# First phase of a fused adaLN transformer block: two row tiles normalized on GpSimd, ScalarE's sum ahead of a copy, first query weights in two transfers

## The chip, the cores and the metric

The kernel runs on one core of a Trainium2 chip. The metric is the device time of one execution in microseconds (us). An execution varies from run to run (six runs of the kernel before: 1272.22 to 1273.15 us), so small differences below are means over runs of the same job (the same chip, the same minutes), with two standard errors behind "±". TensorE is called PE, VectorE DVE, ScalarE ACT and GpSimd POOL, as in the profile.

## The reference, cut to what matters

```python
mod = silu(c) @ w_mod                      # sa, ca, ga, sb, cb, gb: six vectors of 1024
h = layernorm(x) * (1 + ca) + sa           # x: 2048 x 1024
x = x + ga * attention(h, k_cache, v_cache, wq, wo)    # 32 query heads, 4 kv heads, last 512 keys
h = layernorm(x) * (1 + cb) + sb
x = x + gb * swiglu(h, w_gate, w_up, w_down)
```

Only the start matters here: before the first query matmul, PE needs x normalized and transposed for the first 512 rows (four row tiles of 128), the vector ca, and query weights. The shift sa is folded in later as a bias.

## The kernel before: the parts concerned

All transfers are issued in this order on one queue (tile `wm` holds columns of w_mod, `wq8`, which the profile prints as `wq`, the query weights of the first eight heads):

```python
for tt in range(QT): load_x(tt)            # 4 x 256 KB
for half in range(DH):
    load_wm(1, half)                       # scale ca: 1 MB
    load_wq8(2 * half)                     # 512 KB
    load_wq8(2 * half + 1)                 # 512 KB
load_wm(0, 0); ...; load_wm(0, 1)          # shift sa: 2 x 1 MB
```

The first phase, with cuts marked:

```python
nc.tensor.transpose(sil_ps, sil_r, ident[0:DT, 0:DT])
nc.scalar.copy(out=siluc, in_=sil_ps)      # silu(c) as a column, for the w_mod matmuls
warm(4)                                    # filler matmuls
...
stats_0(0)                # DVE: mean and variance of row tile 0
act_sum(1)                # ACT: sum of row tile 1
rstd_0(0)                 # ACT
stats_0(2)                # DVE
act_squares(1)            # ACT
warm(3)
xpose_0(0, ln_norm(0))    # DVE normalizes, PE transposes (8 matmuls)
rstd_0(1, 1.0 / D); rstd_0(2)
warm(5)
stats_0(3)
xpose_0(1, ln_norm(1)); xpose_0(2, ln_norm(2))
rstd_0(3)
n3 = ln_norm(3)
mod_cols(1, 0, ca1, True, (0,))            # first columns of ca: 8 matmuls of one column
xpose_0(3, n3)
...                                        # DVE scales h; then query matmuls, first half
mod_cols(1, 1, ca1, True)                  # second half of ca, after 20 query matmuls
...
q0(1, (6, 7)); sa_mm(0, (0, 1)); q0(2, (6, 7)); sa_mm(0, (2, 3)); sa_out(0)
q0(3, (6, 7)); sh_mm(0, range(5)); q0(4, (6, 7)); sh_mm(0, (5, 6))
sa_mm(1, (0,)); q0(5, (6, 7)); sa_mm(1, (1, 2, 3)); sa_out(1)   # shift sa
```

The order of every engine's instructions in this phase is pinned.

Of the kernel before, what the change touches and what calls it, by code (L numbers as in the profile page):

```python
# [9 lines left out]
ALU = mybir.AluOpType  # L10
AX = mybir.AxisListType
BF16 = mybir.dt.bfloat16
# [576 lines left out]
def fast_path(ctx, tc, flag, A_x, A_k_cache, A_v_cache, A_wq, A_wo, B_x, B_w_gate, B_w_up,  # L589
# [3 lines left out]
    nc = tc.nc  # L593
    P = 128
    _, S, D = A_x.shape
# [23 lines left out]
    wq_v = A_wq.rearrange("(dt p) n -> p dt n", p=P)  # L619
# [15 lines left out]
    wk = ctx.enter_context(tc.tile_pool(name="work", bufs=2))  # L635
# [7 lines left out]
    def blkB(name, shape, dt=BF16):  # L643
        return pb_.tile(shape, dt, name=name, tag="B")
# [4 lines left out]
    def mm(name, shape=(P, 512), dt=FP32):  # L649
        return psp.tile(list(shape), dt, name=name, tag="mm", bufs=4)  # L650

    def big(name, shape=(P, 2, 512), dt=FP32):
        return psp.tile(list(shape), dt, name=name, tag="s", bufs=2)
# [6 lines left out]
    def pin(ins, what="steps"):  # L660
        return tc.keep_in_program_order(ins) if stage[what] else ins

    def fetch(out, in_):
        pin(nc.sync.dma_start(out=out, in_=in_), "dma")

    def load(out, in_):
        with nc.allow_non_contiguous_dma(reason="weight slice"):
            fetch(out=out, in_=in_)
# [18 lines left out]
    xt = [xpool.tile([P, D], BF16, name=f"x{tt}", tag=f"x{tt}") for tt in range(S // P)]  # L687
# [21 lines left out]

    def load_wq8(i):  # L710
        t = blkB("wq8", [P, 2, 8 * P])
        load(t, wq_v[:, 2 * i:2 * i + 2, 0:8 * P])
        wq8.append(t)

    for tt in range(QT):
# [1 line left out]
    for half in range(DH):  # L717
        load_wm(1, half)
        load_wq8(2 * half)
        load_wq8(2 * half + 1)  # L720
# [35 lines left out]
    def warm(n):  # L756
        for _ in range(n):
            nc.tensor.matmul(warm_ps, lhsT=ones_bf, rhs=warm_w, start=True, stop=True)
# [15 lines left out]
    siluc = const.tile([P, DT], BF16, name="siluc")  # L774
    sil_ps = mm("sil_ps", (P, DT), BF16)
    nc.tensor.transpose(sil_ps, sil_r, ident[0:DT, 0:DT])
    nc.scalar.copy(out=siluc, in_=sil_ps)
    warm(4)

    def mod_cols(vec, half, dst, add_one, tiles=(0, 1, 2, 3)):  # L780
# [59 lines left out]
    ln = {}  # L840

    def ln_stats(tt, late=None):
        st = sm.tile([P, DH, nc.vector.BN_STATS_DIM], FP32, name="st", tag="st")
        for i in range(DH):
            pin(nc.vector.bn_stats(out=st[:, i, :], in_=xt[tt][:, i * 512:(i + 1) * 512]))  # L845
        if late is not None:
            nc.vector.bn_aggr(out=late[:, 0:2], in_=st)
            return
        mv = sm.tile([P, 4], FP32, name="mv", tag="mv", bufs=4)
        nc.vector.bn_aggr(out=mv[:, 0:2], in_=st)  # L850
        nc.scalar.activation(out=mv[:, 2:3], in_=mv[:, 1:2], func=ACT.Ln, bias=eps_t)
        nc.scalar.activation(out=mv[:, 2:3], in_=mv[:, 2:3], func=ACT.Exp, scale=-0.5)
        ln[tt] = mv

    def ln_norm(tt, on_act=False, n=None):
        mv = ln.pop(tt)
        n = wk.tile([P, D], BF16, name="xn", tag="xn", bufs=3) if n is None else n
        if on_act:
            nc.vector.scalar_tensor_tensor(out=mv[:, 3:4], in0=mv[:, 0:1], scalar=-1.0,
                                           in1=mv[:, 2:3], op0=ALU.mult, op1=ALU.mult)  # L860
            nc.scalar.activation(out=n, in_=xt[tt], func=ACT.Identity, bias=mv[:, 3:4],
                                 scale=mv[:, 2:3])
        else:
            pin(nc.vector.tensor_scalar(out=n, in0=xt[tt], scalar1=mv[:, 0:1],
                                        scalar2=mv[:, 2:3], op0=ALU.subtract, op1=ALU.mult))
        return n

    xn = {}
# [89 lines left out]
    def xpose_0(t, n):  # L958
        for dt in range(DT):
            nc.tensor.transpose(h0_ps[dt // 4][:, dt % 4, t * P:(t + 1) * P],  # L960
                                n[:, dt * P:(dt + 1) * P], ident)

    def rstd_0(t, sums=1.0):
        mv = ln[t]
        nc.scalar.activation(out=mv[:, 2:3], in_=mv[:, 1:2], func=ACT.Ln, bias=eps_t, scale=sums)
        nc.scalar.activation(out=mv[:, 2:3], in_=mv[:, 2:3], func=ACT.Exp, scale=-0.5)

    def stats_0(t):
        mv = ln[t] = sm.tile([P, 4], FP32, name="mv", tag="mv", bufs=4)
        ln_stats(t, mv)  # L970

    def act_sum(t):
        mv = ln[t] = sm.tile([P, 4], FP32, name="mv", tag="mv", bufs=4)
        junk = wk.tile([P, D], BF16, name="junk", tag="junk", bufs=1)
        nc.scalar.activation(out=junk, in_=xt[t], func=ACT.Identity, accum_out=mv[:, 3:4])

    def act_squares(t):
# [3 lines left out]
        nc.scalar.activation(out=junk, in_=xt[t], func=ACT.Square, bias=mv[:, 0:1], scale=-1.0,  # L981
                             accum_out=mv[:, 1:2])

    stats_0(0)
    act_sum(1)
    rstd_0(0)
    stats_0(2)
    act_squares(1)
    warm(3)
    xpose_0(0, ln_norm(0))  # L990
    rstd_0(1, 1.0 / D)
    rstd_0(2)
    warm(5)
    stats_0(3)
    xpose_0(1, ln_norm(1))
    xpose_0(2, ln_norm(2))
    rstd_0(3)
    n3 = ln_norm(3)
# [63 lines left out]
    for i in range(2):  # L1062
        t = big("q_ps")
# [228 lines left out]
    for tt in range(QT, S // P):  # L1292
        cc, t = divmod(tt, QT)
# [98 lines left out]
    for cc in range(NTC):  # L1392
# [3 lines left out]
        for fg in range(NFG):  # L1396
            n = cc * NFG + fg + 1
# [32 lines left out]
def kernel(tc, *args):  # L1430
    nc = tc.nc
    with tc.tile_pool(name="guard", bufs=1) as gp:
        flag = gp.tile([1, 1], I32, name="flag")
        over = fast_path(tc, flag, *args)
        with tc.If(over > 0):
            general_path(tc, *args)
# [30 lines left out]
```

## Time and profile before

| | before |
|---|---|
| median of 3 runs | 1272.88 us |
| span of the profiled run | 1271.2 us |
| PE busy | 1263.8 us |
| tile 2 of x lands; first half of the ca columns lands | 6.07; 9.77 us |
| first query matmul | 12.12 us |
| first score matmul (phase over, PE packed from here) | 30.61 us |

A landing is the last of the sixteen completion records of a transfer in the trace. The timeline's columns are start, duration, engine, line, operation, tiles and shapes, count and, in brackets, the idle time in front and what ended it. The places where PE first meets a large transfer look like this:

```profile
10.81 0.30 PEld L785 LDWEIGHTS <-wm 128*128 128x128 bf16 x8
12.12 4.60 PE L1032 MATMUL q_ps<-hs,wq 128*128 128x512 bf16 x20
16.34 1.06 PEld L785 LDWEIGHTS <-wm 128*128 128x128 bf16 x32
22.75 0.67 PEld L1050 LDWEIGHTS <-wm 128*128 128x128 bf16 x16
30.61 0.59 PE L1197 MATMUL s_ps<-qT,kT 128*128 128x512 bf16 x2
```

No bracket says "<-DMA". PE meets each of these tiles after it has landed.

### The profile page before, as it was taken

How to read it: one execution, taken by the hardware profiler on the slowest of the kernel's cores; microseconds unless marked ns; L12 is line 12 of the kernel's file. 1: busy time of each engine (PE TensorE's matmuls, PEld its weight loads, DVE VectorE, ACT ScalarE, POOL GpSimd, SP SyncE). 2: the span in 40 equal slices, each digit the busy share in tenths (PEclk: the TensorE clock that was granted, in tenths of full speed). 3: DMA queues.
4: the chain of work that ended last, by engine and by line, in shares of the span. 5: the costliest groups of instructions: out<-in, count | busy, mean ns of one | idle time of the engine just before them, and what ended most of it. 6: DMA issues, size and time to landing. Idle time of an engine off the chain costs nothing.

```text
span 1271.2 us, 18164 instructions
## 1 busy us (share of the span) xinstructions
PE 1263.8 (99%) x7589; PEld 641.3 (50%) x7589; DVE 609.8 (48%) x1334; ACT 335.6 (26%) x440; POOL 1.4 (0%) x11
## 2 busy tenths in 40 slices
PE   9999999999999999999999999999999999999998
PEld 4555555555555555555554444444444444444444
DVE  5666658885678665567564631321122112221122
ACT  3643334343333433334341111011100111011100
POOL 0000000000000000000000000000000000000000
PEclk9999999999999999999999999999999999999999
DMA  9897656779557655455575478336633565425702
GB/s 291 205 250 176 173 141 155 185 159 217 127 137 173 152 137 154 113 154 108 125 202 147 133 227 250 95 94 209 213 116 105 168 210 185 158 91 168 246 19 67
DMA packets 306844, 204.46 MB, mean 161 GB/s; under 512 B 145601, under 2 KB 303297, under 8 KB 306754
## 3 DMA queue, kind: packets, MB, share of 16 engines
q1 hardware_dynamic: 301842, 199.03, 58.0%
q10 hardware_dynamic: 4912, 4.20, 1.0%
q8 instruction: 61, 1.00, 0.3%
q14 instruction: 29, 0.24, 0.1%
HBM read 165.94 MB, written 4.21 MB: 134 GB/s over the span
## 4 chain that ended last, share of the span: by engine, by line
PE 97%; DVE 2%; DMA 0%; SPq 0%; issue 0%
PE gu_ps L1343 30%; PE a_ps L1261 17%; PE q_ps L1186 16%; PE d_ps L1363 15%; PE o_ps L1229 9%; PE s_ps L1197 8%; PE q_ps L1032 1%; DVE st L845 0%; DMA x<-in_A_x_dram 0%; DVE junk L1120 0%; DVE junk L816 0%; DVE oq L1216 0%; DVE qT L946 0%; DVE f L1274 0%; DVE f L1273 0%; DVE x L1276 0%
## 5 line engine op out<-in xcount | busy, mean ns | idle before, releaser
L1199 ACT ACTIVATE pT<-s_ps 128x1024 bf16<-128x1024 f32 x256 | 249.2, 1020 | 345.0 <-PE s_ps L1197 344.9
L1261 PE MATMUL a_ps<-wo,oT 128*128 128x512 bf16 x1024 | 241.9, 379 | 0.0
L1186 PE MATMUL q_ps<-hT,wq 128*128 128x512 bf16 x960 | 227.1, 379 | 0.0
L1349 DVE TENSOR_TENSOR guT<-gu_ps,sg 128x512 bf16<-128x512 f32 x112 | 77.5, 692 | 287.5 <-ACT sg L1348 287.5
L1343 PE MATMUL gu_ps<-hT,wg 128*128 128x512 bf16 x896 | 211.7, 379 | 0.0
L1348 ACT ACTIVATE sg<-gu_ps 128x512 bf16<-128x512 f32 x112 | 66.9, 597 | 488.6 <-PE gu_ps L1343 480.1
L1363 PE MATMUL d_ps<-wd,guT 128*128 128x512 bf16 (+2 forms) x952 | 194.2, 366 | 0.0
L1343 PE MATMUL gu_ps<-hT,wu 128*128 128x512 bf16 x672 | 163.3, 379 | 0.0
L1261 PEld LDWEIGHTS <-oT 128*128 128x128 bf16 x1024 | 100.2, 98 | 120.6
L946 DVE CAST qT<-q_ps 128x512 bf16<-128x512 f32 x121 | 83.6, 691 | 151.7 <-PE q_ps L1186 151.4
L1186 PEld LDWEIGHTS <-wq 128*128 128x128 bf16 x960 | 93.9, 98 | 113.0
L1363 PEld LDWEIGHTS <-guT 128*128 128x128 bf16 x952 | 90.9, 98 | 103.0
L1229 PEld LDWEIGHTS <-pT 128*128 128x128 bf16 x2048 | 126.6, 98 | 30.5 <-issue 0.4
L1343 PEld LDWEIGHTS <-wg 128*128 128x128 bf16 x896 | 87.6, 98 | 105.5
L1229 PE MATMUL o_ps<-v_sb,pT 128*128 128x130 bf16 x2048 | 137.0, 220 | 0.1
L1197 PE MATMUL s_ps<-qT,kT 128*128 128x512 bf16 x512 | 131.6, 379 | 0.0
L1343 PEld LDWEIGHTS <-wu 128*128 128x128 bf16 x672 | 65.8, 98 | 79.3
L1216 DVE TENSOR_TENSOR oq<-o_ps,rl 128x256 bf16<-128x256 f32 (+2 forms) x256 | 100.5, 420 | 3.9
L1367 DVE TENSOR_TENSOR f<-d_ps,gb_bc 128x512 f32<-128x512 f32 (+2 forms) x34 | 22.5, 660 | 140.1 <-PE d_ps L1363 140.1
L1197 PEld LDWEIGHTS <-kT 128*128 128x128 bf16 x512 | 44.9, 98 | 31.2 <-issue 0.5
L1269 DVE TENSOR_TENSOR acc<-a_ps,acc 128x512 f32<-128x512 f32 x64 | 44.0, 688 | 32.6 <-PE a_ps L1261 32.6
L1343 PE MATMUL gu_ps<-hT,v_sb 128*128 128x512 bf16 x224 | 57.5, 379 | 0.0
(99 smaller groups left out, 426.4 us busy)
## 6 DMA issues: line engine op xcount, KB each, us to landing
wq<-in_A_wq_dram SPq DMA_DIRECT2D x64, 512.0 KB
wo<-in_A_wo_dram SPq DMA_DIRECT2D x64, 512.0 KB
wg<-in_B_w_gate_dram SPq DMA_DIRECT2D x56, 512.0 KB
wd<-in_B_w_down_dram SPq DMA_DIRECT2D x56, 512.0 KB
wu<-in_B_w_up_dram SPq DMA_DIRECT2D x42, 512.0 KB
v_sb<-in_B_w_up_dram SPq DMA_DIRECT2D x14, 512.0 KB
x<-in_A_x_dram SPq DMA_DIRECT2D x16, 256.0 KB
wm<-in_w_mod_dram SPq DMA_DIRECT2D x4, 1024.0 KB
```

Source lines behind the costliest of these rows:

```text
L946: nc.vector.tensor_copy(out=t, in_=q_ps)
L1186: nc.tensor.matmul(q_ps, lhsT=w, rhs=hT[("h1", cc)][:, dt, :], start=(dt == 0), stop=(dt == DT - 1))
L1197: nc.tensor.matmul(s_ps[:, i, :], lhsT=kT[:, kv, j * P:(j + 1) * P], rhs=qT[g], start=True, stop=True)
L1199: nc.scalar.activation(out=p[:, 2 * jj:2 * jj + 2, :], in_=s_ps, func=ACT.Exp, scale=scale)
L1216: nc.vector.tensor_tensor(out=dst, in0=ps[:, s0:s0 + cnt, 0:Dh], in1=sc, op=ALU.mult)
L1229: nc.tensor.matmul(o_slot["ps"][:, s_, :], lhsT=pT[g][:, j, t * P:(t + 1) * P], rhs=v_sb[:, kv, j, 0:VN], start=(j == 0), stop=(j == WT - 1))
L1261: nc.tensor.matmul(a_ps, lhsT=oT[(cc, 2 * q + i)][:, hh % 4, t * P:(t + 1) * P], rhs=wo_tiles[(cc, q, dh, i)][:, hh % 4, :], start=(hh == ...
L1269: nc.vector.tensor_tensor(out=acc[(cc, t)][:, dsl], in0=a_ps, in1=acc[(cc, t)][:, dsl], op=ALU.add)
L1343: nc.tensor.matmul(ps[:, n, :], lhsT=gu_w[(cc, fg, nm, dt // 4)][:, dt % 4, fi * P:(fi + 1) * P], rhs=hT[("h2", cc)][:, dt, :], start=(dt ...
L1348: nc.scalar.activation(out=g, in_=ps[:, 0, :], func=ACT.Silu)
L1349: nc.vector.tensor_tensor(out=guT[(cc, fg)][:, fi, :], in0=ps[:, 1, :], in1=g, op=ALU.mult)
L1363: nc.tensor.matmul(d_ps, lhsT=guT[(cc, f // 4)][:, f % 4, t * P:(t + 1) * P], rhs=wd_tiles[(cc, dh, f // 4)][:, f % 4, c0:c0 + w], start=( ...
```

## The change

DVE works through statistics and normalizations of four row tiles while POOL is idle. The change gives two of the normalizations to POOL, lets ACT start its sum before it waits for PE's silu(c), and cuts the first 512 KB of query weights in two so that PE can start on the first half.

```diff
     def load_wq8(i):
         t = blkB("wq8", [P, 2, 8 * P])
-        load(t, wq_v[:, 2 * i:2 * i + 2, 0:8 * P])
+        for j in range(2 * i, 2 * i + 2) if i == 0 else ():
+            load(t[:, j % 2, :], wq_v[:, j, 0:8 * P])
+        if i > 0:
+            load(t, wq_v[:, 2 * i:2 * i + 2, 0:8 * P])
 ...
-    nc.scalar.copy(out=siluc, in_=sil_ps)
     warm(4)
 ...
+    def norm_0(t):
+        mv = ln[t]
+        n = wk.tile([P, D], BF16, name="xn", tag="xn", bufs=3)
+        nc.gpsimd.tensor_scalar(out=mv[:, 3:4], in0=mv[:, 0:1], scalar1=-1.0, scalar2=1.0,
+                                op0=ALU.mult, op1=ALU.mult)
+        nc.gpsimd.tensor_scalar(out=n, in0=xt[t], scalar1=mv[:, 3:4], scalar2=mv[:, 2:3],
+                                op0=ALU.add, op1=ALU.mult)
+        return n
 ...
     act_sum(1)
+    nc.scalar.copy(out=siluc, in_=sil_ps)
 ...
-    xpose_0(0, ln_norm(0))
+    xpose_0(0, norm_0(0))
 ...
-    xpose_0(1, ln_norm(1))
+    xpose_0(1, norm_0(1))
```

## The prediction

> **What bounds the kernel now.** I read the page first, then the list of waits, then the timeline of the first 32 us, because the diff touches nothing after that. The page says that TensorE (PE) is busy almost everywhere, and the chain of work that ended last is almost all PE:
>
> ```profile
> PE 1263.8 (99%) x7589; PEld 641.3 (50%) x7589; DVE 609.8 (48%) x1334; ACT 335.6 (26%) x440; POOL 1.4 (0%) x11
> ...
> PE 97%; DVE 2%; DMA 0%; SPq 0%; issue 0%
> ```
>
> So 1271.2 - 1263.8 = 7.4 us of the span is all that PE does not fill. The 2% of DVE in the chain is not slack to be had everywhere: it lies at the start and at the very end. A change in the first phase can win only what makes the first query matmul (q_ps on tile hs) start sooner, and what PE then keeps. The chain in order of time shows the start:
>
> ```profile
> 1.67 4.40 DMA x<-in_A_x_dram
> 6.07 0.02 issue
> 6.09 1.30 DVE st L845 x2
> 7.39 0.02 issue
> 7.41 0.21 DVE mv L847
> 7.62 0.41 DVE xn L864
> 8.03 1.21 DVE st L845 x2
> 9.24 0.02 issue
> 9.26 0.04 DVE mv L847
> 9.30 0.09 issue
> 9.39 0.52 DVE xn L864
> 9.91 0.05 issue
> 9.95 1.08 PE h_ps L960 x16
> 11.03 0.18 PE mod_ps L785 x8
> 11.21 0.47 PE h_ps L960 x8
> 11.68 0.58 PE mod_ps L785 x24
> 12.26 4.46 PE q_ps L1032 x20
> ```
>
> The reader is to see that, from the landing of tile 2 of x at 6.07 to the transposes at 9.95, VectorE (DVE) does statistics and normalizations one after the other; only then does PE run as a chain. The first 4.6 us of it are the wait for x, which no part of the change touches. The timeline shows what DVE does there, columns start, duration, engine, line, operation:
>
> ```profile
> 7.54 0.49 DVE L864 TENSOR_SCALAR xn<-x,mv 128x1024 bf16<-128x1024 bf16 x1
> 7.95 1.28 DVE L845 BATCH_NORM_STATS2 st<-x 128x6 f32<-128x512 bf16 x2
> 9.26 0.21 DVE L847 BATCH_NORM_AGGREGATE mv<-st 128x2 f32<-128x12 f32 x1
> 9.39 1.42 DVE L864 TENSOR_SCALAR xn<-x,mv 128x1024 bf16<-128x1024 bf16 x3
> ```
>
> Row tile 0 is normalized ahead of tile 3's statistics, and tile 1 ahead of tiles 2 and 3. GpSimd (POOL) is idle all that time.
>
> The other side is DMA: in the windows from 4.4 to 23 us its share is 1.00 or more, at 349 to 373 GB/s. The completion records of the trace, last of sixteen per transfer, give the landings: x tile 1 at 3.94, tile 2 at 6.07, tile 3 at 6.73, scale columns wm (first half) at 9.77, first query weights at 11.28, second 12.69, second half of wm 15.66, the shift's two wm tiles 22.03 and 25.14. PE first uses these at 10.81, 12.10, about 13.5 (after six matmuls), 16.34, 22.75 and 25.91. **Each transfer that PE meets has only about 0.7 us in hand.**
>
> **What the Trainium skill says.** "GPSIMD Engine Reference", section 3.1, puts elementwise work with at most two operations and one input at 1.03 cycles an element at 1.2 GHz, a good unrolled loop at 1.8, two inputs at 2.6. For 1024 elements that is an estimate of 0.88, 1.54 or 2.2 us, plus dispatch. The trace before has no comparable instruction; POOL's 8x128 product took 0.42 us. "SBUF — State Buffer", section "Who interferes with whom", says that a DVE tensor_scalar in a two-port mode and a GpSimd instruction exclude each other, while DVE work with one SBUF input outside those modes does not contend. The normalizations (1024 elements in about 0.5 us, so over one element a cycle) are in such a mode by that page; the statistics (512 in 0.68 us) show one element or less. No overlap exists in the trace before. "TensorE: Matmul & The Clock Gate", Part 1, says that PE starts at half clock for a run-variable few microseconds: the trace agrees, the filler matmuls start 0.45 us apart until about 7.2 us and 0.22 to 0.25 after.
>
> **The change part by part.**
>
> *ScalarE order.* The sum of tile 1 (1.06 us) starts at 4.53 now, because ahead of it the copy of silu(c), 0.17 us, waited 1.29 us for PE. Tile 1 is there at 3.94, so the sum can start at about 3.96. The copy then follows, so rstd of tile 0 is ready 0.57 - 0.17 = 0.4 us sooner: 5.7 instead of 6.10. The squares and rstd of tile 1 move as well: ready at about 7.65 instead of 8.03. siluc itself comes at 5.2, long before its first reader at 10.8.
>
> *Rows 0 and 1 on GpSimd.* Adds two tiny negations (estimate 0.2 us each; the first one hides behind ScalarE's rstd) and two passes over 128x1024. I take 1.1 us each, the port-bound figure above plus about 0.2 of dispatch. Row 0: 5.8 to 6.9. Row 1 waits for its rstd at 7.65: 7.7 to 8.8. PE's filler (seven matmuls at half clock) ends at 7.44, so transposes of row 0 start at 7.45 instead of 8.09; five fillers (1.1 us) then run to 9.0, and row 1's transposes follow at once instead of at 9.95. By then neither is on the path.
>
> *DVE.* Loses two passes. Statistics of tile 3 start at 7.54 right behind tile 2's (now 7.95): 0.41 us. They and their aggregate end so that row 2 starts at 8.98 instead of 9.85 (the second of the three in the 9.39 group): 0.41 + 0.46 = 0.87 us sooner. Row 3 needs rstd of tile 3: the aggregate's start moves from 9.26 to 8.85, ScalarE's two steps from 9.50 to about 9.1, ready 9.63; row 3 is done at 10.18 instead of 10.81.
>
> *PE behind it.* Row 2's transposes 9.55 to 10.0; the first eight scale-column matmuls follow (wm landed 9.77, so just in time); row 3's transposes start at about 10.23 instead of 11.07. Gain here 0.84 us, and the scale of hs follows in the same spacing: first query matmul at about 11.28 instead of 12.12.
>
> *Weights in two pieces.* The first 256 KB hold all that the first three matmuls read. An x tile of that size took about 0.65 us, so it lands at 10.4 to 10.6 and the second at 11.28, as before. Without the split the 512 KB land at 11.28, which is just when hs is ready: the split is worth 0 to 0.1 us. It adds one issue on SP, off the path because the DMA queue is backed up.
>
> *What PE keeps.* With everything 0.84 us earlier, PE asks for the second half of wm at 15.50, which lands at 15.66 plus a few hundredths: kept gain 16.34 - 15.71 = 0.63. For the shift tiles: 22.75 - 22.08 = 0.67, 25.91 - 25.19 = 0.72, so these no longer cost more. The later kT lands at about 27.5 against a first use at 30.4. Sum: **-0.63 us**, rounded to -0.6, and PE stays the bound for the other 1240 us, where loads are issued by the release of buffers and move along with PE. 1272.88 - 0.6 = 1272.3 us.
>
> **Rivals.**
>
> 1. *GpSimd is slower than I take.* At 1.54 us plus dispatch, row 1 ends at about 9.4; row 2 on DVE would be blocked by the shared port from 8.98 to 9.4, row 3 ends near 10.5, the gain at the first query matmul is 0.5 us. At 2.2 us plus dispatch, row 0 ends at 8.1 and row 1 at 10.5, rows 2 and 3 are pushed to about 11.5, and the kernel loses some 0.4 us: 1273.3. For it: the 0.42 us for 128 elements is slow. Against: that one has two inputs, and the loop runs over one input with two operations.
> 2. *The gain is hidden by DMA.* The landings set a floor: if they come 0.3 us later in the run (the last of sixteen is over 1 us behind the first in each transfer, and a lagging DMA engine need not be the same), the kept gain falls to 0.3 us; if earlier, up to 0.84 us. That makes 1272.0 to 1272.6.
> 3. *The clock gate moves.* Fewer or shifted idle gaps of PE (0.65 us before the first transposes now) cannot cost much, but if full clock came 1 us later, the transposes would wait for fillers and the gain would be gone: about 1272.9.
>
> **Range and chances.** 60% for the 1.1 us pass (1271.9 to 1272.5), 25% for the middle case (1272.3 to 1272.7), 15% for the slow one (1273 to 1273.6). The three runs before spread over 0.63 us, which adds 0.3 either way. Predicted 1272.3, range 1271.7 to 1273.2. Two per cent are 25 us, over three times all of PE's idle time, so "faster" needs what does not exist, and a loss of 25 us would need waits far beyond this phase: 0.003 and 0.007.
>
> **What would show it right or wrong.** Right: POOL has two TENSOR_SCALAR passes of about 1.1 us before 9 us; ScalarE's sum starts near 4.0; statistics of tile 3 near 7.5; first q_ps matmul at 11.2 to 11.5; and PE waits a tenth or two for DMA ahead of the second-half mod_ps matmuls near 15.6, which it does not do now. Wrong: POOL passes of 2 us or more with DVE's row 2 late behind them (rival 1); a first q_ps matmul early but the score matmuls no earlier than 30.6 - 0.3 (rival 2); filler matmuls 0.45 us apart beyond 8 us (rival 3). The step I trust least is the GpSimd duration, next the DMA landings. It would be wrong as a whole if x landed differently in the changed kernel, since all of the chain hangs on tile 2 of x.

## The result, and the profile after

| | before | after |
|---|---|---|
| median, 6 runs each | 1272.87 us (1272.22 to 1273.15) | 1272.97 us (1272.72 to 1273.24) |
| ratio, 95% interval | | 1.0001 (0.9989 to 1.0014): same |
| first query matmul, profiled run | 12.12 us | 11.48 us |
| first score matmul, profiled run | 30.61 us | 30.34 us |

A ratio is the mean time of one kernel's runs over that of the other's of the same rounds, so not quite the ratio of the medians. The time did not move, although the start of the phase did. The page's line of busy times answers to the first of the prediction's, and the chain that ended last, in order of time (start, duration, piece), to its second fence:

```profile
PE 1263.9 (99%) x7589; PEld 641.3 (50%) x7589; DVE 608.6 (48%) x1332; ACT 335.6 (26%) x440; POOL 4.2 (0%) x15
```

```profile
5.89 1.25 ACT junk L983 x2
...
7.86 1.21 POOL xn L991
9.06 0.05 issue
9.11 1.15 PE h_ps L962 x16
10.25 0.18 PE mod_ps L787 x8
10.43 0.61 PE h_ps L962 x8
11.04 0.58 PE mod_ps L787 x24
11.62 1.32 PE q_ps L1044 x6
12.94 0.02 issue
12.96 3.19 PE q_ps L1044 x14
```

POOL is busy 4.2 us instead of 1.4, and the chain to the transposes now runs over ACT's squares and POOL's second pass where it ran over DVE. It also has a break at 12.94 that the chain before did not have: there PE had come to the second transfer of query weights, which landed at 12.91. The timeline of the changed kernel shows both; first the normalizations of the four row tiles, two on each engine, and the first query matmul:

```profile
5.93 1.20 POOL L991 TENSOR_SCALAR xn<-x,mv 128x1024 bf16<-128x1024 bf16 x1 [0.73 <-POOL mv L989]
...
7.86 1.20 POOL L991 TENSOR_SCALAR xn<-x,mv 128x1024 bf16<-128x1024 bf16 x1 [0.57 <-POOL mv L989]
...
9.08 0.49 DVE L866 TENSOR_SCALAR xn<-x,mv 128x1024 bf16<-128x1024 bf16 x1
...
9.82 0.55 DVE L866 TENSOR_SCALAR xn<-x,mv 128x1024 bf16<-128x1024 bf16 x1 [0.25 <-ACT mv L968]
...
11.48 4.67 PE L1044 MATMUL q_ps<-hs,wq 128*128 128x512 bf16 x20
```

Tile 2 of x landed at 6.22 in this run, 0.15 us later than before, and still the first query matmul came 0.64 us earlier. Then, in the same view, the brackets that were missing before:

```profile
12.95 0.98 PEld L1044 LDWEIGHTS <-wq 128*128 128x128 bf16 x6 [0.51 <-DMA wq<-in_A_wq_dram]
...
15.96 0.89 PEld L787 LDWEIGHTS <-wm 128*128 128x128 bf16 x32 [0.30 <-DMA wm<-in_w_mod_dram]
...
22.54 0.47 PEld L1062 LDWEIGHTS <-wm 128*128 128x128 bf16 x16 [0.47 <-DMA wm<-in_w_mod_dram]
```

A bracket counts the idle time of the weight loader, not PE's loss; the loss is read by laying the matmuls of the two traces side by side. The changed kernel's are 0.64 us ahead at the first query matmul and 0.45 at the seventh, the first to read the second query weights. At the thirteenth 0.55 is back, since the kernel before had a pause of its own there. The wait for the second half of ca costs PE nothing (0.56 on both sides of it). The lead is 0.41 after the first half of sa and 0.28 after the second. From there to the last of the 7589 matmuls it stays 0.28 us. Nothing after 30 us gives or takes anything.

### The profile page after: what moved, and what is told of

It reads as the page before. It is cut to its first block, busy times and chain, and to the rows that moved or that the text cites. A ratio compares the mean times of both kernels' runs of the same rounds, so it can differ in the third digit from the quotient of the medians.

```text
span 1271.0 us, 18169 instructions
## 1 busy us (share of the span) xinstructions
PE 1263.9 (99%) x7589; PEld 641.3 (50%) x7589; DVE 608.6 (48%) x1332; ACT 335.6 (26%) x440; POOL 4.2 (0%) x15
## 4 chain that ended last, share of the span: by engine, by line
PE 97%; DVE 1%; ACT 0%; DMA 0%; POOL 0%; issue 0%; SPq 0%
PE gu_ps L1355 30%; PE a_ps L1273 17%; PE q_ps L1198 16%; PE d_ps L1375 15%; PE o_ps L1241 9%; PE s_ps L1209 8%; PE q_ps L1044 1%; DVE junk L1132 0%; DMA x<-in_A_x_dram 0%; DVE st L847 0%; DVE junk L818 0%; DVE oq L1228 0%; DVE qT L948 0%; DVE f L1286 0%; PE one_ps L1062 0%; DVE f L1285 0%
```

## The experiments

Twelve runs were made (two of them of the unedited kernels), each with five timed runs and one profile, in three jobs of four. Besides these there is the job of the result, so "before" stands for four sets of 6, 9, 14 (nine, and the five of *before_again*) and 9 runs, with means of 1272.78, 1273.00, 1272.70 and 1272.90 us. Since these move by 0.3 us, each kernel is compared within its job.

### no_split: one transfer for the first query weights again

```diff
 # against the changed kernel
-        for j in range(2 * i, 2 * i + 2) if i == 0 else ():
-            load(t[:, j % 2, :], wq_v[:, j, 0:8 * P])
-        if i > 0:
-            load(t, wq_v[:, 2 * i:2 * i + 2, 0:8 * P])
+        load(t, wq_v[:, 2 * i:2 * i + 2, 0:8 * P])
```

> The changed kernel with the first query weights in one transfer again. Theory S (the split itself slows the DMA queue): in the changed kernel's profile the 2 KB packets of the first query weights took 139 to 220 ns between 7.5 and 9.5 us, against 84 to 91 in the kernel before, and every later landing was 0.22 to 0.47 us later; without the split the first-half packets are back near 85 ns, the second half of wm lands near 15.66 and the last wm tile near 25.14, so PE's score matmuls start 0.6 us ahead of the kernel before (29.8) and the time is about 0.3 us below the changed kernel's. Rival G (GpSimd's second pass, 7.86 to 9.06, disturbs the transfers) and rival C (chance from run to run): the landings stay about as late as in the changed kernel, or as spread, and nothing is gained, within 0.15 us.

Measured: median 1272.49 us (1272.40 to 1272.96), 0.43 ± 0.29 us below the kernel before of its job. The profile's lead over the kernel before is 0.83 us after the second half of ca and 0.63 us at the score matmuls, and it stays to the end. In its timeline only one bracket still names a transfer of weights:

```profile
22.20 0.46 PEld L1059 LDWEIGHTS <-wm 128*128 128x128 bf16 x16 [0.40 <-DMA wm<-in_w_mod_dram]
```

This speaks against POOL's passes alone as the cause (rival G): they are in this kernel too (at 5.96 and 7.89, 1.19 us each), and it gains. The packets of the first query weights before 10.1 us took 84 to 93 ns in the median of each quarter, as expected.

### after_again: the changed kernel, unedited

> The changed kernel, unedited, for a second profile. Theories S and G both expect the slow 2 KB packets (over 130 ns before 9.5 us) to come again and the last wm tile to land at 25.4 to 25.8; rival C expects a different landing, 25.0 to 25.4, with packets near 85 ns. Time within 0.15 us of the kernel before or up to 0.3 below it.

Measured: median 1272.98, 0.10 ± 0.39 below the kernel before of its job; over the two jobs the changed kernel is 0.04 ± 0.26 us above it, so nothing. The slow packets came again (76 of 256 over 130 ns), and the last wm tile landed at 25.54. The first query matmul stood at 11.14, as tile 2 of x landed at 5.63. Even so the lead over the first profile of the kernel before was only 0.33 us at the score matmuls. The weight loader waited for the second piece of query weights, the next query weights, the second half of ca and the first half of sa, but PE lost most of its lead at one of them:

```profile
13.12 3.19 PE L1044 MATMUL q_ps<-hs,wq 128*128 128x512 bf16 x14 [0.53 <-DMA wq<-in_A_wq_dram]
```

The lead was 0.98 us up to there, 0.29 behind it, and 0.40 from the thirteenth query matmul on, before and after ca. The second half of sa took the last 0.06.

### slack and slack_no_split: PE meets the wm tiles later

```diff
             q0(g, range(4))
-        if i == 0:
-            mod_cols(1, 1, ca1, True)
-            ...
+            if g == 2:
+                mod_cols(1, 1, ca1, True)
+                ...
 ...
     q0(1, (6, 7))
+    q0(2, (6, 7))
     sa_mm(0, (0, 1))
-    q0(2, (6, 7))
+    q0(3, (6, 7))
     sa_mm(0, (2, 3))
     sa_out(0)
-    q0(3, (6, 7))
-    sh_mm(0, range(5))
     q0(4, (6, 7))
-    sh_mm(0, (5, 6))
+    sh_mm(0, range(7))
 ...
-    sa_mm(1, (0,))
     q0(5, (6, 7))
-    sa_mm(1, (1, 2, 3))
+    sa_mm(1, (0, 1, 2, 3))
```

> The changed kernel with PE's use of the second half of wm moved four query matmuls later (0.86 us) and of both shift tiles two later (0.43 us); the work is the same. Theory F (the arrival of the wm tiles is the floor that takes PE's lead of 0.64 us down to 0.28): PE keeps 0.55 to 0.64 us, score matmuls start near 29.8, time 0.3 us below the changed kernel. Rival L (the lead is lost in the phase itself, in DVE's and ScalarE's steps around the scales and shifts, or later): no gain over the changed kernel, score matmuls near 30.1.

> Both edits: PE's later use of the wm tiles, and one transfer for the first query weights. Theory F with S: the same 0.6 us below the kernel before as with the later use alone, since no wm tile is waited for in either; a wait for the first query weights of 0.1 us at most may appear. Rival L: as the changed kernel. If the first query weights land at 11.3 or later the first query matmul stands at 11.4 or later, not 11.48 as in the changed kernel minus anything.

Measured: slack 1272.74 us median, but 1272.40 to 1274.80; slack_no_split 1274.05, from 1272.15 to 1274.86. Both expectations fell. In four of the ten runs the reason is in neither theory. The reordering puts 28, 32 and 28 matmuls of one column close together with only four 512-column ones between. In the profiled run of slack_no_split (1274.86 us) the table by windows shows what happened. Its columns are the window, busy time and count of PE, of its weight loader, of DVE, ACT and POOL, then the granted clock, the DMA share and GB/s:

```profile
26.00:28.00 2.00, 2.00 (x49) 1.36 (x47) 1.09 (x5) 0.26 (x1) 0.00 (x0) 1.00 0.71 139
28.00:30.00 2.00, 2.00 (x32) 1.16 (x32) 1.68 (x5) 2.00 (x4) 0.00 (x0) 0.68 1.90 278
30.00:32.00 2.00, 2.00 (x6) 0.71 (x5) 2.00 (x4) 0.41 (x1) 0.00 (x0) 0.50 0.63 109
```

PE was busy all the time by this view, yet it fell to half clock; the clock records put it from 28.72 to 32.13, which is 3.41 us. At half clock that costs about 1.7 us, and the profile agrees: PE was 0.15 us behind the kernel before ahead of this stretch and 1.84 us behind it after. A mean clock of 0.998 over the run marks such an execution: three of five runs of slack_no_split (1274.05 to 1274.86) and one of five of slack (1274.80) have it, and no run of any other kernel here. The Trainium skill, "TensorE: Matmul & The Clock Gate", Part 1, speaks of a free-running window of 4096 cycles, 3413 ns, and of idle PE; the length agrees with this trace, and so does the "free-running" (only some runs are hit). No idle time shows ahead of it, but the ends of matmuls are modelled in the profile, so short pauses of PE need not show. That narrow matmuls are the cause is not shown: the kernel before has the same 88 of them between 24.80 and 28.46 us, with six wide ones between instead of four, and none of its runs is hit.

So the times of these two do not test the floor. The profile of slack does, since that run (1272.85 us) had full clock. PE met the second half of ca without a wait, as intended, yet the score matmuls came at 30.53 and not near 29.8, because PE waited for query weights, which theory F had left out:

```profile
13.03 4.06 PE L1044 MATMUL q_ps<-hs,wq 128*128 128x512 bf16 x18 [0.43 <-DMA wq<-in_A_wq_dram]
```

Of a lead of 0.98 us at the first query matmul 0.38 was left here, 0.49 from the thirteenth on, 0.15 after a wait for the next query weights at 18.92, and 0.08 at the score matmuls. The four runs of slack at full clock have a mean of 1272.64, 0.36 ± 0.28 below the kernel before; they were picked after the fact.

The floor also begins earlier than I had it: in the profile of slack_no_split the first half of ca landed at 10.86 us, after PE wanted it.

```profile
10.91 0.35 PE L784 MATMUL mod_ps<-siluc,wm 128*128 128x1 bf16 x8 [0.83 <-DMA wm<-in_w_mod_dram]
```

### split_only, pool_only, act_only: one part of the change alone

Each is the kernel before with one of the three parts of the diff above.

> The kernel before with the split of the first query weights alone. Theory S (the split itself slows its own 2 KB packets; 76 and 85 of 256 took over 130 ns in two profiles of the changed kernel, 45, 41 and 0 in three profiles with one transfer): 55 or more slow packets before 10.3 us although GpSimd is idle, the last piece landing at 11.4 to 11.8, the last wm tile at 25.3 or later; the time the same or up to 0.2 us above the kernel before, whose PE has 0.7 us in hand. Theory G (GpSimd's pass is the cause): 45 slow packets or fewer, the last wm tile near 25.1, no change of time.

> The kernel before with rows 0 and 1 on GpSimd alone. Theory: this is the part that makes the lead; with ScalarE's sum still late (4.53) rstd of row 1 comes at about 8.0, GpSimd's second pass ends at 9.25, its transposes start at 9.3 instead of 9.1, the first query matmul at 11.5 to 11.7, and PE keeps 0.4 to 0.6 us to the end: 0.2 to 0.5 us below the kernel before. Rival: the order on ScalarE is needed and this alone gives under 0.2 us.

> The kernel before with ScalarE's sum ahead of its copy alone. Theory: nothing, within 0.15 us: row 0's normalization on DVE still waits for the statistics of tile 2, which wait for x, so an earlier rstd is not used; the first query matmul stays near 12.1 if x lands as before. Rival: DVE gets row 1's rstd earlier and something moves by 0.3 us.

| kernel | median us | mean against before of its job | tile 2 of x lands | first query matmul | first score matmul |
|---|---|---|---|---|---|
| split_only | 1273.09 | +0.26 ± 0.31 | 6.25 | 12.30 | 30.80 |
| pool_only | 1272.72 | +0.12 ± 0.27 | 5.75 | 11.60 | 30.09 |
| act_only | 1272.79 | +0.06 ± 0.22 | 5.46 | 11.51 | 30.16 |

None is faster; pool_only was expected to be 0.2 to 0.5 us faster and is not. Its profile is 0.52 us ahead of the kernel before, but 0.32 of this is tile 2 of x, which landed earlier. The profile of act_only seems to contradict its own time: its first query matmul is 0.61 us ahead of the kernel before. But tile 2 of x landed 0.61 us earlier in that run. In this kernel, in split_only and in the kernel before, the first query matmul stands 6.05 us behind that landing, three times the same; ACT's order alone is worth nothing, as expected. One profile per kernel misleads as long as such landings are not taken out.

In pool_only the distance is 5.85 us, and what holds it is the chain over ACT: row tile 1 lands at 4.15, and the query matmul comes 7.45 us behind that. With ACT's order added it is 7.14 or 7.15 in after_again and no_split. So by the profiles the ACT part is worth 0.3 us at the first query matmul, but only together with the POOL part.

split_only missed its number of slow packets (39 of 256 over 130 ns, where 55 were expected), so the explanation by slow packets falls; see the end of this section.

### before_again: the kernel before, unedited

> The kernel before, unedited, for a second profile: shows how far landings and the first query matmul move from run to run. Theory: last wm tile at 25.0 to 25.6, first query matmul 11.7 to 12.3, depending on when tile 2 of x lands, time within 0.15 us of the kernel before. Slow 2 KB packets of the first query weights: 50 or fewer if the split is the cause of more.

Measured: median 1272.77. Tile 2 of x landed at 5.62, but the first query matmul came only at 12.22, because the first half of ca landed at 10.82:

```profile
10.87 0.35 PE L785 MATMUL mod_ps<-siluc,wm 128*128 128x1 bf16 x8 [0.28 <-DMA wm<-in_w_mod_dram]
```

So even the kernel before is sometimes held by this transfer. It also had 74 slow packets with one transfer, more than expected: the split is not what makes packets slow.

### no_split_again, and three runs with lighter shift tiles

The first is the kernel of no_split a second time. The other three load half of each sa tile and use it twice (wrong), with the instructions on all engines unchanged:

```diff
-    load_wm(0, 0)
+    load_wm(0, 0, DT // 2)            # the same for load_wm(0, 1)
 ...
-    lhsT=wm_tiles[(0, half)][:, dt, i * P:(i + 1) * P]
+    lhsT=wm_tiles[(0, half)][:, dt % 4, i * P:(i + 1) * P]
```

> The changed kernel with one transfer for the first query weights, a second time: its first five runs had median 1272.49, the changed kernel's eleven a mean near 1272.94, those of the kernel before near 1272.85. If the split is what takes the gain, the median is again 1272.3 to 1272.65, 0.2 to 0.5 us below the kernel before of this job. If the first five were chance: 1272.75 to 1273.0.

> Wrong result on purpose (the shift of the first layer norm is computed from half of its weights, used twice; same instructions on every engine). The kernel before with half the bytes in both shift transfers, so that they land about 1.5 and 3 us sooner. Theory F (the wm landings are a floor only for a kernel that runs ahead): no change for the kernel before, within 0.2 us of it, apart from runs in which these tiles came late. Control of the next two.

> Wrong result on purpose, as the run before it. The changed kernel with half the bytes in both shift transfers. Theory F: no wait for the shift tiles near 22.5 and 25.6; PE keeps what it has after the second half of wm (0.56 and 0.40 us in two profiles), so the time is 0.1 to 0.3 us below the changed kernel's 1272.94 and below light_before. Rival: the same time as the changed kernel, within 0.1 us; then the landings of the shift tiles were no floor.

> Wrong result on purpose, as the two before it. The changed kernel with one transfer for the first query weights and half the bytes in both shift transfers: every cause named is taken away. Theory F with S: the whole lead is kept, 0.6 to 0.8 us below light_before, about 1272.1 to 1272.3. If it stays at the 1272.5 of the kernel without the split, the shift tiles are not what is left.

| kernel | median us | mean against before of its job | first half of ca lands | first query matmul |
|---|---|---|---|---|
| no_split_again | 1272.60 | -0.33 ± 0.26 | 10.14 | 11.53 |
| light_before | 1273.08 | +0.14 ± 0.27 | 9.54 | 11.98 |
| light_shift | 1272.80 | -0.15 ± 0.24 | 10.31 | 11.62 |
| light_no_split | 1272.59 | -0.26 ± 0.34 | 10.40 | 11.80 |

The gain without the split is repeated; over its two jobs no_split is 0.38 ± 0.19 us faster than the kernel before. It is the version that beats both, by 0.03%.

Lighter sa tiles do nothing for the kernel before, as expected. Under the changed kernel they give 0.29 ± 0.23 us against light_before, where the change with its full tiles gives 0.04 ± 0.26 in the other direction: in the expected direction, but the intervals overlap. No wait for a sa tile is left in either of the last two profiles. light_no_split stays at 1272.59, no better than no_split_again of its job (0.07 ± 0.33), and 0.40 ± 0.33 below light_before where 0.6 to 0.8 was expected: so the sa tiles are not what is left. The profiles of light_shift and light_no_split say where the rest stayed. The waits for DMA have moved to the front; in the window of the first 31 us of light_shift (engine, what it does and what it waited for, us in total, times, longest) they are these:

```profile
PEld L1044 <- DMA wq<-in_A_wq_dram: 0.7, 1, 0.7
PEld L787 <- DMA wm<-in_w_mod_dram: 0.5, 2, 0.3
PE q_ps L1044 <- DMA wq<-in_A_wq_dram: 0.2, 1, 0.2
```

The query weights and ca, not sa. In light_no_split the profile has besides a single wait for query weights at 75.5 us, far behind the phase, that cost some 0.47 us (from the first score matmul to the last matmul it takes 1236.06 us, the kernel before 1235.59); whether it comes in every run the profile cannot tell.

### What fourteen profiles together show

The kernel before and the changed one were profiled with the result, and the twelve runs add one profile each. From the first score matmul to the last matmul it is 1235.58 to 1235.60 us in thirteen of the fourteen (1236.06 in light_no_split), so what separates these runs lies in the first phase. The first half of ca, last of sixteen records, landed between 9.10 and 10.86 us over these fourteen, although the same bytes stand in front of it in all. The first query matmul followed this landing by 1.31 to 1.41 us in all five profiles in which the first ca matmuls came right behind it (before_again, slack_no_split, no_split_again, light_shift, light_no_split). Without such a wait it comes 6.04 or 6.05 us behind tile 2 of x in the kernels with DVE alone. With all of POOL's and ACT's part it came 5.26 us behind tile 2 where that landed late (the profile of the result), and 7.14 or 7.15 us behind tile 1 where it landed early (after_again, no_split, slack).

The mean of the sixteen records, which one lagging DMA engine moves less than the last does, gives the split's price: from the first half of ca to the second half, with the same bytes between, it is 5.99 us in the nine profiles with one transfer (5.72 to 6.28) and 6.41 in the five with two (6.10 to 6.66). That is 0.42 us more on the queue that PE waits for. But the four of the five that have POOL's passes give 6.25 to 6.66; split_only, which has not, gives 6.10, within the four profiles that have neither (5.96 to 6.28). Whether the split costs this by itself or only beside POOL's passes is open: one profile is too few. In times the split costs +0.34 ± 0.39, +0.26 ± 0.31 and +0.10 ± 0.31 in the three pairs that differ by it alone (the changed kernel against no_split, split_only against before, light_shift against light_no_split), 0.23 ± 0.20 in the mean. How two transfers take longer than one stays open: slow packets are as many in some runs without it.

The port to SBUF that DVE and POOL share can be seen as well. In slack, row 2's normalization starts on DVE at 8.03 while POOL's pass runs to 8.93, and takes 1.18 us instead of 0.49. In the six profiles with such an overlap (slack, no_split_again, no_split, after_again, slack_no_split, pool_only) it ended 0.27 or 0.28 us behind POOL's end, whenever it had started.

## Why the prediction was right or wrong

The time, 1272.97 us, lies in the range and is "same" as expected; the value of 1272.3, that is the gain of 0.6 us, did not come. The range was wide enough to hold no gain at all, so that the time fell into it says nothing for the mechanism; of the three cases that got chances (1271.9 to 1272.5, 1272.3 to 1272.7, 1273 to 1273.6) none holds it.

- **The trade between engines: right.** POOL's passes took 1.20 us, predicted 1.1; ACT's sum started at 4.14, predicted about 4.0; the first query matmul came 5.26 us behind tile 2 of x, predicted 5.21 (11.28 - 6.07), against 6.05 before. Rival 1, a slow POOL, did not take place, nor did rival 3: full clock began at 6.21 us against 7.21 before, and at 4.52 to 7.22 over the fourteen profiles. One piece was wrong: rows 0 and 1 were to be off the path. In after_again, no_split and slack the first query matmul hangs on tile 1 of x, ACT's squares and POOL's second pass.
- **The port: right.** The page on SBUF that the prediction names states an exclusive lock, and the six overlaps above agree with it, as far as they go: 0.28 us behind POOL's end is less than the 0.49 of a pass alone, so some part of it had passed before. The prediction took the two-port mode from the rate of the normalizations, which alone does not show it; the overlaps do. It cost PE nothing that I see: in after_again, no_split, slack and pool_only PE ran the sixteen transposes of rows 1 and 2 as one group, 1.07 us in each.
- **"Weights in two pieces": this step failed.** It counted 0 to 0.1 us of gain and no cost, with the first piece at 10.4 to 10.6 and the second at 11.28. They landed at 10.86 and 11.55, everything behind them was late, and the kernel without it is the one that gains, 0.38 us. In its place the runs show a cost of 0.2 to 0.4 us (0.23 ± 0.20 in the mean of the paired times, 0.42 in the records of landings), with the open question named above. The Trainium skill, "SBUF — State Buffer", section "Summary: rules for kernel authors", advises 128 partitions and one DMA, not several, for a transfer that bounds; the prediction did not use it, and the runs agree with it.
- **"What PE keeps": this step failed too.** Its sum of -0.63 us took the landings of one profile as fixed times. They are not: the first half of ca moves within 1.76 us from run to run. Where it came at 10.14 or later in a kernel with POOL's part, or at 10.82 in the kernel before, it and not DVE set the first query matmul. The slack of 0.7 us in the profile before was true of that run (and of the last three transfers; the first two had 1.04 and 0.82). The step took the second half of ca as the first limit, and its wait did come, but cost PE nothing in the two profiles of the changed kernel. It left out the second query weights: they were listed with 13.5 against 12.69, 0.8 us in hand, and the lead of 0.84 us used that up. The weight loader waited for them in seven of the nine profiles of kernels with POOL's part, all but no_split and pool_only. They cut the lead from 0.64 to 0.45 in the profile of the result and from 0.98 to 0.29 in after_again.
- **Rival 2, the gain hidden by DMA, is what happened,** more strongly than it said: it gave 0.3 us of kept gain as its worst case, which is what the two profiles of the changed kernel show (0.28 and 0.33), while the times of eleven runs show 0.04 ± 0.26 us in the other direction. The two agree: the profiled executions are timed too, and took 1273.01 us before and 1272.77 and 1272.68 after, so 0.24 and 0.33 less. But the one before was 0.18 slower than the mean of its 38 runs in these jobs, and the two after about 0.2 faster than that of their eleven. The leads are those of chosen executions and not of the mean.
- **The later 1240 us: right.** The lead at 30 us is the lead at the end.
- **Small misreadings.** The wait for x is 4.40 us in the chain shown, not 4.6; the filler matmuls start 0.43 us apart and then 0.21 to 0.22, not 0.45 and 0.22 to 0.25. Nothing hangs on them.

## What to carry to other kernels

Before work is taken off an engine at the start of a kernel, list the landings of every transfer that the bound engine meets later, from several profiles, since the smallest distance in hand caps the gain and one run's distance is not a constant. Take a split of a transfer for what it costs the queue, not only for what its first half frees. And look at every run's clock after regrouping narrow matmuls: four of ten runs of the two regrouped kernels lost theirs, for a reason that is not shown.

## What the Trainium skill lacked or had wrong

- "TensorE: Matmul & The Clock Gate", Part 1, ties the return to half clock to idle time of PE. In slack_no_split PE had none from 24 to 28.7 us by the profile (whose ends of matmuls are modelled), but 88 of its matmuls from 25.4 us had one column, and it ran at half clock from 28.72 to 32.13; four of ten runs of the two regrouped kernels show it, at 1274.05 to 1274.86 us against 1272.15 to 1272.85 of the others. How matmuls of one column count for the clock no page says.
- "GPSIMD Engine Reference", section 3.1, has figures for fp32 and cycles per element; a bf16 normalization of 128x1024 with two operations and two per-row operands took 1.19 to 1.20 us on POOL in all nine profiles that have it, against 0.49 on DVE.
- No page that I found gives the run-to-run spread of a landing: the same transfer behind the same bytes landed between 9.10 and 10.86 us in fourteen profiles.
